# Reordering vector work and two state reads in a fused mLSTM and GELU kernel

## Chip, cores and metric

One Trainium2 chip, one core. The metric is the device time of one execution in microseconds (us); the median of 3 runs of the kernel before is 484.98 us (482.9 to 485.1). Engines are named as in the profile: PE is TensorE's matrix multiply, PEld its weight load, DVE VectorE, ACT ScalarE, POOL GpSimd, SP SyncE, whose queue starts all the transfers here.

## What is computed

The reference runs an mLSTM cell over q, k, v of shape (4, 8, 768, 40) with three gates, and feeds its output to a two-layer block with an exact GELU. Everything is float32.

```python
for t in range(S):                       # S = 768
    m_new = maximum(f + m, i)            # f, i: gates at t
    C = exp(f + m - m_new) * C + exp(i - m_new) * outer(v_t, k_t)
    n = exp(f + m - m_new) * n + exp(i - m_new) * k_t
    y[:, :, t] = sigmoid(o_t) * (C @ q_t) / maximum(abs(n . q_t), 1)
x = y.transpose(0, 2, 1, 3).reshape(3072, 320)
h = x @ w_in                             # 320 -> 2048
out = (0.5 * h * (1 + erf(h / sqrt(2)))) @ w_out   # 2048 -> 320
```

## The kernel before

**Chunks and stages.** The 768 steps are cut into NCH = 6 chunks of 128 steps; one chunk holds 4 batches b = 0 to 3 of 8 heads. Within a chunk the cell is a small attention: scores k·q, multiplied by a decay mask W that ACT makes with an exponential, times v (`values`), plus the carried state read with q and scaled by gT (`far`), and at the end of the chunk an update of the state. The 512 rows of x of a chunk then go through the up product into the hidden g (2048 x 512) and through the down product into the output.

After a front part (`FRONT`, to about 129 us) the kernel runs five stages, c = 1 to 5. Stage c does `up` for chunk c and then plays the order string `DOWN`: the 14 pieces of the down product of chunk c, mixed with the cell of chunk c + 1. The last stage has down pieces alone. The order is written by hand: each word of `DOWN` is a letter and a batch, and emits its instructions on the engines at that place. Each engine runs its own instructions strictly in that order.

**Letters** of `DOWN` that matter here:

- `F`: the next of 14 down pieces, 8 matmuls each (L888). Two pieces share one right-hand side. The scheme needs fewer than 16 products because sums of blocks of g stand in for blocks of g. Pieces 3 and 4 use the sums s2, pieces 7 and 8 the sums s1.
- `S0`, `S2`: scores of batches 0, 1 and of batches 2, 3 (`scores_two`): 64 small matmuls (L523) and 8 DVE multiplies of the scores into W (L529).
- `K`, `Q`: DVE transposes of k and q (L455); after `Q` the next batch's k and q are fetched by 16 transfers (L157), and POOL weighs v (L494).
- `C0`, `C2`: `carry_two`: 64 matmuls that read the state with q (L578), 32 that make its update (L585), then DVE's scaling of what was read (L594), POOL's decay of the state (L598) and DVE's addition of the update (L599).
- `V`: values (L617) and DVE's addition of them to what was read (L625). `V` of a batch loads W as weights, even heads first, odd heads after.
- `Y`: the division of the output by its norm (L630 on POOL, L632 to L635 on DVE). `X`: transposes of the output into x (L652), which need a copy of its last 64 columns, doubled (`y_rest`, L641); the copy for the next batch is made by DVE once `X` of this batch has read the present one. `R`: DVE splits x into two parts (L670, L671).
- `N`: `sum_late`, two DVE subtractions of 128x1024 that turn a block of g into a block difference (L918). It may run only after pieces 5 and 6 have read the block, and pieces 11 and 12 need it.
- `Z`: one step of the last weight sum T4, two DVE subtractions of 128x160 (L726); there are four, in stage 1 alone. Pieces 13 and 14 use T4.
- `M`, `W`, `G`, `L`, `D`, `B`, `j`: masks on POOL, exponentials and sigmoids on ACT, loads.

**up.** Four `pair` calls, 0 to 3, make the hidden pieces from x in three weight parts: w_hi, w_lo and their sum w_mid, which DVE joins anew in each stage (`join_weight`, L716). Each pair multiplies with w_hi, w_lo and w_mid in that order (L812); `rest` adds the last 64 rows of x (L823). ACT applies the GELU (L827). `hidden_sums(g, f0, f1)` is three DVE operations of 128x512 (L744 to L746) that form s1, s2 and a difference. After the GELUs of pairs 0 and 1 it is called for 0 to 2 and for 2 to 4; pair 3 then joins weights 8 and 9, and, in its `ahead` step, weight 7, which `rest(1, ...)` needs. One kind of joined weight (`w_in_mid`) has its own small buffers, so that the join for pair 3 may have to wait for an earlier pair's matmuls.

Of the kernel before, what the change touches and what calls it, by code (L numbers as in the profile page):

```python
# [9 lines left out]
F32 = mybir.dt.float32  # L10
# [6 lines left out]
P = 128  # L17
# [14 lines left out]
    Y1 T3 J J U U S3 V2 K K J G3 J Y2 C3 X0 K V3 J K F J F K K B8 F J K F F J K F F F R0 X1 J J K F J F K X2 F J K F  # L32
    J Y3 K F R1 J F Z B9 B10 F X3 R2 Z R3 F p"""
DOWN = """
    M0 Z M1 W0 F L3 F B3 W1 Z Z S0 F K2 C0 M2 G0 G1 G2 G3 V0 V1 W2 F Q2 K3 Q3 Y0 M3 D3 F F W3 F S2 F C2 V2 V3 j Z N F Y1
    X0 R0 Y2 F F X1 Y3 R1 F X2 R2 F X3 R3 F"""


@with_exitstack
def kernel(  # L40
# [18 lines left out]
    B, H, S, D = q.shape  # L59
    L = P  # L60
    NCH = S // L
    NP = H // 2
    D1 = D + 1
# [22 lines left out]
    ps_h = ctx.enter_context(tc.tile_pool(name="ps_h", bufs=2, space=bass.MemoryType.PSUM))  # L86
# [75 lines left out]
    def turn_of(n):  # L162

        return n % NLD if n < 2 * B else (n - 2 * B) % NQ
# [224 lines left out]
    def per_head(t, c, b):  # L389
        return t[:, c, b * H:(b + 1) * H].unsqueeze(2)  # L390

    class Cell:
# [173 lines left out]

            self.read(b)

        def carry_two(self, b0):

            c, two_b = self.c, (b0, b0 + 1)
            banks = [ps_h.tile([P, H + NP, D1], F32, name="pf", tag="h") for _ in range(2)]
            for i, b in enumerate(two_b):
                qT = self.qT.pop(b)
                for p in range(NP):
                    for r in halves:
                        for hip in range(2):
                            nc.tensor.matmul(banks[hip][r, NP * i + p, :], qT[halves[hip], p, r],  # L578
                                             state[b][halves[hip], p, 0:D1], start=True, stop=True)
            if c + 1 < NCH:  # L580
                for i, b in enumerate(two_b):
                    vw = self.vw.pop(b)
                    for p in range(NP):
                        for hip in range(2):
                            nc.tensor.matmul(banks[i][halves[hip], H + p, :], kb[turn_of(c * B + b)][:, 2 * p + hip, :],  # L585
                                             vw[:, 2 * p + hip, :], start=True, stop=True)
            for i, b in enumerate(two_b):
                if b == B - 1:
                    self.far[b] = qb[2].rearrange("p h d -> p (h d)")[:, 0:H * D1].rearrange("p (h d) -> p h d", d=D1)
                else:  # L590
                    self.far[b] = fars[0].tile([P, H, D1], F32, name="far", tag="hs", bufs=2)
                by_hip = lambda t, hip: t.rearrange("p (m two) d -> p m two d", two=2)[:, :, hip, :]
                for hip in range(2):
                    nc.vector.tensor_tensor(out=by_hip(self.far[b], hip), in0=banks[hip][:, NP * i:NP * i + NP, :],  # L594
                                            in1=by_hip(per_head(gT, c - 1, b), hip).to_broadcast([P, NP, D1]), op=OP.mult)
                if c + 1 < NCH:
                    st, d = state[b][:, :, 0:D1], dec[:, c - 1, b * NP:(b + 1) * NP].unsqueeze(2).to_broadcast([P, NP, D1])
                    nc.gpsimd.tensor_tensor(out=st, in0=st, in1=d, op=OP.mult)  # L598
                    nc.vector.tensor_tensor(out=st, in0=st, in1=banks[i][:, H:H + NP, :], op=OP.add)  # L599
                self.read(b)  # L600
# [113 lines left out]
    def join_weight(i):  # L714
        w_mid[i] = raw.tile([P, 2, WP // 2], F32R, name="w_in_mid", tag="pow") if i % 5 in (1, 4) else w_f(F32R, "w_mid")
        nc.vector.tensor_tensor(out=w_mid[i], in0=w_hi[i], in1=w_lo[i], op=OP.add)  # L716
# [22 lines left out]
    def hidden_sums(g, f0, f1):  # L739

        (a11, a21), (_, a22) = [[g.t[:, HF * e + f0:HF * e + f1, HT * h:HT * (h + 1)] for h in range(2)]
                                for e in range(2)]
        s1, s2 = [t[f0 // (HF // 2)][:, f0 % (HF // 2):f0 % (HF // 2) + f1 - f0, :] for t in (g.s1, g.s2)]
        nc.vector.tensor_tensor(out=s1, in0=a21, in1=a22, op=OP.add)  # L744
        nc.vector.tensor_tensor(out=s2, in0=s1, in1=a11, op=OP.subtract)
        nc.vector.tensor_tensor(out=a21, in0=a11, in1=a21, op=OP.subtract)  # L746
# [44 lines left out]
    def up(g, sums_too, turns):  # L791

        def split_to(i):
            while len(w_lo) <= i:
                split_weight()

        def pair(f, ahead):

            at = [f // 2 * 5 + f % 2 * 3 + x for x in range(NX)]
            split_to(at[1])  # L800
            for i in at:
                if i not in w_mid:
                    join_weight(i)
            pus = [[pool.tile([P, TG], F32, name="pu", tag=tag) for e in range(2)]
                   for pool, tag in (((ps_h, "h"), (ps_mm, "a")), ((ps_tr, "tr"), (ps_mm, "b")))[f % 2]]
            ahead()
            mid = [w_mid.pop(i) for i in at]
            for n, (w, x) in enumerate((([w_hi[i] for i in at], parts["x"]), ([w_lo[i] for i in at], parts["x_lo"]), (mid, parts["x_all"]))):
                for i in range(2):
                    for e in range(2):  # L810
                        for k in range(NX):
                            nc.tensor.matmul(pus[i][e], w[k][:, e, i * P:(i + 1) * P], x[:, k, :],  # L812
                                             start=(n == 0 and k == 0), stop=False, skip_group_check=True)
            return pus

        def rest(u, banks, order):
            mid = w_mid.pop(5 * u + 2)
            for i in order:
                pu = banks[i]
                for n, (w, x) in enumerate(((w_hi[5 * u + 2], parts["x"]), (w_lo[5 * u + 2], parts["x_lo"]), (mid, parts["x_all"]))):  # L820
                    for e in range(2):
                        r = halves[e]
                        nc.tensor.matmul(pu[e], w[r, i // 2, i % 2 * P:(i % 2 + 1) * P], x[r, NX, :], start=False,  # L823
                                         stop=(n == 2), skip_group_check=True)

        def out(i, e, pu):
            nc.scalar.activation(out=g.t[:, HF * e + i, :], in_=pu[e], func=AF.Gelu, scale=4097.0)  # L827

        b0 = pair(0, lambda: split_to(4))
        b1 = pair(1, lambda: join_weight(2))  # L830
        for step in turns[:1]:
            step()
        rest(0, b0 + b1, (0, 1, 2, 3))
        split_to(6)
        join_weight(5)
        join_weight(6)
        for i, pu in enumerate(b0 + b1):
            for e in range(2):
                out(i, e, pu)
        for step in sums_too[:5]:  # L840
            step()
        b2 = pair(2, lambda: split_to(9))
        hidden_sums(g, 0, 2)
        hidden_sums(g, 2, 4)
        b3 = pair(3, lambda: join_weight(7))
        for step in turns[1:] + sums_too[5:]:
            step()
        rest(1, b2 + b3, (2, 3, 0, 1))
        for i, e in ((2, 0), (2, 1), (3, 0), (0, 0), (1, 0), (3, 1), (0, 1), (1, 1)):
            out(4 + i, e, (b2 + b3)[i])  # L850
        hidden_sums(g, HF - 2, HF)
        hidden_sums(g, HF - 4, HF - 2)
# [100 lines left out]
    def cell_steps(c, letters, before=None):  # L953
        cell = Cell(c)
        cell.before = before
        return dict(zip(letters, (cell.mask, cell.weights, cell.gate, cell.turn, cell.scores, cell.carry, cell.values,
                                  cell.finish, cell.turn_y, cell.split_x, cell.load_last, cell.turn_k,
                                  cell.turn_q, cell.weigh_last, cell.carry_two,
                                  cell.last_M, cell.scores_two, cell.load_next)))

    first_g = Hidden(False)
    n_pieces = range(len(pieces))
# [8 lines left out]
    for c in range(1, NCH):  # L971
        g, later, steps = Hidden(True), [], {}
        if c + 1 < NCH:
            steps = cell_steps(c + 1, "MWGTscVYXRLKQDCBSj", g)
        up(g, weight_sum(1) + weight_sum(2) + weight_sum(3) if c == 1 else [], [lambda b=b: (steps["K"](b), steps["Q"](b)) for b in range(2)] if steps else [])
        if c == 1:
            later = weight_sum(4)
        products, late = down_steps(c, g)
        steps |= dict(F=in_turn(products), Z=in_turn(later), N=late)
        play("F " * 14 if c + 1 == NCH else DOWN, steps)  # L980
# [30 lines left out]
```

## Time and profile before

| | |
|---|---|
| median of 3 runs | 484.98 us (482.9 to 485.1) |
| profiled execution, own time | 483.16 us |
| its span, first to last instruction | 481.2 us |
| PE matmul / weight load busy | 473.1 us / 410.8 us |
| DVE / ACT / POOL busy | 351.5 / 222.2 / 73.7 us |
| granted TensorE clock | 1.000 |

Stages of the profiled execution, from the chain of waits (start of the up product, start of the first down piece, end), in us from the span's start:

| stage c | up starts | down starts | down ends | up | down |
|---|---|---|---|---|---|
| 1 | 129.33 | 158.27 | 203.07 | 28.94 | 44.80 |
| 2 | 203.07 | 231.65 | 275.89 | 28.58 | 44.24 |
| 3 | 275.89 | 304.48 | 348.39 | 28.59 | 43.91 |
| 4 | 348.39 | 376.99 | 418.85 | 28.60 | 41.86 |
| 5 | 418.85 | 447.43 | 478.07 | 28.58 | 30.64 |

Stages 1 to 3 hold the same number of matmuls; stage 4 lacks the 64 of the state update. An idle time in the profile is put down to the instruction that ended it ("PEld px L652 <- DVE y_rest L641" is PE's weight load waiting for a DVE copy). Ends of matmuls are modelled, so starts of weight loads are the better clock for PE.

### The profile page before, as it was taken

Reading aid. Unit: us, or ns where it says so; the run is one execution under the profiler, and the core shown is the slowest. Engines: PE = TensorE matmul, PEld = TensorE weight load, DVE = VectorE, ACT = ScalarE, POOL = GpSimd, SP = SyncE. Lnnn points to the kernel's source line nnn. Section 1 sums busy time; section 2 is a strip of 40 time slices with the busy share of each in tenths; the row PEclk is TensorE's granted clock in tenths of the full one; section 3 lists DMA queues with packets and bytes.
Section 4 is the critical chain, followed back from the end, with each engine's and each line's share of the span. In section 5 each row is a group of like instructions: output and inputs, shape, how many; then the busy total and the mean of one; then the engine's idle time right before and its main releaser. Section 6 shows DMA issues by size and latency. Waiting matters only on the chain.

```text
span 481.2 us, 11954 instructions
## 1 busy us (share of the span) xinstructions
PE 473.1 (98%) x4740; PEld 410.8 (85%) x4740; DVE 351.5 (73%) x762; ACT 222.2 (46%) x477; POOL 73.7 (15%) x104
## 2 busy tenths in 40 slices
PE   8899999999999999999999999999999999999997
PEld 7787888877777999877899977899977899977997
DVE  7899689797879988857488857488857488724321
ACT  6977999944532942113952103852104862112300
POOL 3001210000030234200136300135200213000000
PEclk9999999999999999999999999999999999999999
DMA  9998975289420368532257651257651250100001
GB/s 175 192 214 189 188 175 150 77 199 189 133 30 4 40 121 175 92 70 23 31 92 169 86 108 23 29 89 167 99 108 20 34 90 4 51 6 0 1 1 54
DMA packets 170423, 44.49 MB, mean 92 GB/s; under 512 B 156448, under 2 KB 163904, under 8 KB 170368
## 3 DMA queue, kind: packets, MB, share of 16 engines
q1 hardware_dynamic: 170368, 43.73, 46.4%
q8 instruction: 37, 0.61, 0.5%
q14 instruction: 18, 0.15, 0.1%
HBM read 39.58 MB, written 4.13 MB: 91 GB/s over the span
## 4 chain that ended last, share of the span: by engine, by line
PE 87%; DVE 7%; ACT 1%; SPq 1%; DMA 1%; issue 1%; DVEq 0%
PE po L888 30%; PE pu L812 22%; PE po L865 7%; PE pu L757 6%; PE pu L823 6%; PE ph L617 5%; PE ps L523 2%; PE pf L578 2%; PE pu L763 2%; PE px L652 2%; PE pf L585 1%; DVE g L918 1%; PE ps L507 1%; SPq L147 1%; PE pt L481 1%; ACT g L827 1%
## 5 line engine op out<-in xcount | busy, mean ns | idle before, releaser
L888 PE MATMUL po<-w_out,g 128*128 128x160 f32 x640 | 91.6, 301 | 0.0
L888 PEld LDWEIGHTS po<-w_out,g 128*128 128x128 f32 x640 | 87.9, 190 | 2.0 <-ACT g L827 1.8
L827 ACT ACTIVATE g<-pu 128x512 f32<-128x512 f32 x80 | 40.8, 614 | 53.4 <-PE pu L823 53.2
L888 PE MATMUL po<-w_sums,sums 128*128 128x160 f32 x320 | 47.7, 303 | 0.0
L888 PEld LDWEIGHTS po<-w_sums,sums 128*128 128x128 f32 x320 | 44.1, 190 | 0.7
L744 DVE TENSOR_TENSOR sums<-g 128x512 f32<-128x512 f32 x20 | 13.8, 690 | 38.5 <-ACT g L827 38.5
L812 PE MATMUL pu<-x_hi,w_in_hi 128*128 128x512 f32 x160 | 41.7, 403 | 0.0
L662 ACT ACTIVATE x_hi<-px 128x384 fp32r<-128x384 f32 x20 | 9.8, 489 | 67.8 <-PE px L652 67.8
L812 PE MATMUL pu<-x_lo,w_in_lo 128*128 128x512 f32 x160 | 40.6, 395 | 0.0
L432 ACT ACTIVATE W<-W,aT 128x128 f32<-128x128 f32 x128 | 39.2, 389 | 0.1
L812 PEld LDWEIGHTS pu<-x_hi,w_in_hi 128*128 128x128 f32 x160 | 28.5, 188 | 9.4 <-ACT g L827 4.1
L812 PEld LDWEIGHTS pu<-x_lo,w_in_lo 128*128 128x128 f32 x160 | 30.1, 188 | 7.2
L865 PE MATMUL po<-w_out,g 128*128 128x320 f32 x128 | 35.2, 433 | 0.0
L865 PEld LDWEIGHTS po<-w_out,g 128*128 128x128 f32 x128 | 24.0, 190 | 9.5
L827 ACT ACT_TABLE_LOAD x5 | 6.4, 1283 | 55.1 <-PE pu L823 41.3
L812 PE MATMUL pu<-x_all,w_in_mid 128*128 128x512 f32 x80 | 31.7, 396 | 0.1
L812 PE MATMUL pu<-x_all,w_mid 128*128 128x512 f32 x80 | 31.7, 396 | 0.0
L444 POOL MEMSET g<- 32x1024 f32 x8 | 7.6, 944 | 150.0 <-ACT W L432 149.8
L406 POOL TENSOR_SCALAR_AFFINE_SELECT W<-W 128x1024 f32<-128x1024 f32 (+2 forms) x20 | 21.8, 1100 | 55.4 <-DMA W<-M_d 55.1
L901 DVE TENSOR_TENSOR o_sb<-po,o_sb 128x320 f32<-128x320 f32 (+1 forms) x27 | 12.5, 465 | 23.9 <-PE po L888 19.9
L757 PE MATMUL pu<-first_x,w_in 128*128 128x256 f32 x128 | 29.1, 382 | 0.0
L757 PEld LDWEIGHTS pu<-first_x,w_in 128*128 128x128 f32 x128 | 23.8, 190 | 3.5 <-DVE w_in L374 0.4
(183 smaller groups left out, 910.0 us busy)
## 6 DMA issues: line engine op xcount, KB each, us to landing
W<-M_d SPq DMA_DIRECT2D x16, 512.0 KB, 5.7
bits<-in_moe_w_in_dram SPq DMA_DIRECT2D x20, 256.0 KB, 4.3
bits<-in_moe_w_out_dram SPq DMA_DIRECT2D x16, 320.0 KB, 3.2
ob<-in_o_gate_dram SPq DMA_DIRECT2D x24, 160.0 KB, 3.5
out_dram<-o_sb SPq DMA_DIRECT2D x24, 160.0 KB, 2.1
vb<-in_v_dram SPq DMA_DIRECT2D x14, 160.0 KB, 5.0
kb<-in_k_dram SPq DMA_DIRECT2D x14, 160.0 KB, 5.0
g<-M_d SPq DMA_DIRECT2D x4, 512.0 KB, 4.4
```

The source lines that it names most:

```text
L406: nc.gpsimd.affine_select(out=x, in_=x, compare_op=OP.is_ge, fill=1.0e30, base=base, pattern=[[0, H], [1, x.shape[2]]], channel_multiplier=-1)
L432: nc.scalar.activation(out=W[n][:, h, :], in_=src, func=AF.Exp, scale=-1.0, bias=aT[:, self.c, r:r + 1])
L617: nc.tensor.matmul(ph[r, h, :], Pm[:, h, r], vb[turn_of(n)][:, h, :], start=True, stop=True)
L662: nc.scalar.activation(out=parts["x"][:, :, t], in_=px, func=AF.Copy, scale=PART)
L744: nc.vector.tensor_tensor(out=s1, in0=a21, in1=a22, op=OP.add)
L757: nc.tensor.matmul(banks[-1][e][:, i - i0, :], in_tile(i, x)[:, e, i % 2 * P:(i % 2 + 1) * P], first_x[:, x, t0:t1], start=(x == 0 and i = ...
L812: nc.tensor.matmul(pus[i][e], w[k][:, e, i * P:(i + 1) * P], x[:, k, :], start=(n == 0 and k == 0), stop=False, skip_group_check=True)
L823: nc.tensor.matmul(pu[e], w[r, i // 2, i % 2 * P:(i % 2 + 1) * P], x[r, NX, :], start=False, stop=(n == 2), skip_group_check=True)
L827: nc.scalar.activation(out=g.t[:, HF * e + i, :], in_=pu[e], func=AF.Gelu, scale=4097.0)
L865: nc.tensor.matmul(po[b], g.t[:, f, b * L:(b + 1) * L], w_out[:, f, :], start=(f == 0), stop=(f == NF - 1))
L888: nc.tensor.matmul(bank[at][:, i, :], lhs(j, t), rhs(j), start=(first and i == 0 and j == 0), stop=(i == n - 1 and j == HF - 1), skip_grou ...
L901: nc.vector.tensor_tensor(out=to, in0=pb, in1=x, op=OP.add)
```

## The change

Three parts. In `DOWN` the late sums `N` go from behind `j` to ahead of `W3` and `S2`, and the last `Z` goes from ahead of `N` to behind `X1`. `carry_two` is cut into a reading half (`C`) and an updating half (new letter `h`); for batches 0 and 1 the third down piece `F`, which stood between `S0` and `C0`, now stands between `C0` and `h0`; for batches 2 and 3 `h2` follows `C2` directly. In `up` the second `hidden_sums` goes into pair 3's `ahead` step, so that the joins of weights 8 and 9 come ahead of it and the join of weight 7 still behind it.

```diff
 DOWN = """
-    M0 Z M1 W0 F L3 F B3 W1 Z Z S0 F K2 C0 M2 G0 G1 G2 G3 V0 V1 W2 F Q2 K3 Q3 Y0 M3 D3 F F W3 F S2 F C2 V2 V3 j Z N F Y1
-    X0 R0 Y2 F F X1 Y3 R1 F X2 R2 F X3 R3 F"""
+    M0 Z M1 W0 F L3 F B3 W1 Z Z S0 K2 C0 F h0 M2 G0 G1 G2 G3 V0 V1 W2 F Q2 K3 Q3 Y0 M3 D3 F F N W3 F S2 F C2 h2 V2 V3 j F Y1
+    X0 R0 Y2 F F X1 Z Y3 R1 F X2 R2 F X3 R3 F"""
...
-        def carry_two(self, b0):
+        def read_two(self, b0):
...
-            banks = [ps_h.tile([P, H + NP, D1], F32, name="pf", tag="h") for _ in range(2)]
+            banks = self.banks = [ps_h.tile([P, H + NP, D1], F32, name="pf", tag="h") for _ in range(2)]
...
                             nc.tensor.matmul(banks[hip][r, NP * i + p, :], qT[halves[hip], p, r],
                                              state[b][halves[hip], p, 0:D1], start=True, stop=True)
+
+        def update_two(self, b0):
+
+            c, two_b, banks = self.c, (b0, b0 + 1), self.banks
             if c + 1 < NCH:
...
         hidden_sums(g, 0, 2)
-        hidden_sums(g, 2, 4)
-        b3 = pair(3, lambda: join_weight(7))
+        b3 = pair(3, lambda: (hidden_sums(g, 2, 4), join_weight(7)))
```

No instruction is added or removed on any engine. On PE only the eight matmuls of piece 3 change place, on DVE the joins, `N` and one `Z`; the orders on ACT, POOL and SP are the same.

More of the change, by code (lines that the diff above doesn't have):

```diff
@@ L957, in cell_steps @@
                                   cell.finish, cell.turn_y, cell.split_x, cell.load_last, cell.turn_k,
-                                  cell.turn_q, cell.weigh_last, cell.carry_two,
-                                  cell.last_M, cell.scores_two, cell.load_next)))
+                                  cell.turn_q, cell.weigh_last, cell.read_two,
+                                  cell.last_M, cell.scores_two, cell.load_next, cell.update_two)))
     first_g = Hidden(False)
@@ L973 @@
         if c + 1 < NCH:
-            steps = cell_steps(c + 1, "MWGTscVYXRLKQDCBSj", g)
+            steps = cell_steps(c + 1, "MWGTscVYXRLKQDCBSjh", g)
         up(g, weight_sum(1) + weight_sum(2) + weight_sum(3) if c == 1 else [], [lambda b=b: (steps["K"](b), steps["Q"](b)) for b in range(2)] if steps else [])
```

## The prediction

> **What bounds the kernel now.** The page first: PE is busy for nearly the whole span, and the chain that ended last is mostly PE.
>
> ```profile
> PE 473.1 (98%) x4740; PEld 410.8 (85%) x4740; DVE 351.5 (73%) x762; ACT 222.2 (46%) x477; POOL 73.7 (15%) x104
> ...
> PE 87%; DVE 7%; ACT 1%; SPq 1%; DMA 1%; issue 1%; DVEq 0%
> ```
>
> As no matmul is removed, the change can only take out places where PE waits. The waits of the weight loads, with total, count and longest in us, bound that from above:
>
> ```profile
> PEld pu L812 <- ACT g L827: 4.1, 17, 0.4
> PEld pu L823 <- issue: 3.7, 10, 0.4
> ...
> PEld pf L578 <- issue: 1.4, 8, 0.2
> PEld px L652 <- DVE y_rest L641: 1.3, 3, 0.8
> ```
>
> The first two are GELU outputs and a change of shape that the change leaves alone. The last two it touches. A third is only in the answer for the joining line L716, as who waited for it:
>
> ```profile
> PEld pu L812: 0.7, 2
> ```
>
> Where do these lie? The stage table says that stage 1 is longer than stage 3 by 28.94 - 28.59 = 0.35 us in the up part and 44.80 - 43.91 = 0.89 us in the down part, stage 2 by 0.33 us in the down part. So 1.57 us is what bringing stages 1 and 2 to stage 3 is worth. The timeline of DVE and of the weight loads shows the down part's cause, in stages 1 and 2:
>
> ```profile
> 187.50 0.50 DVE L625 TENSOR_TENSOR qb<-ph,qb 128x328 f32<-128x328 f32 x1 [0.19 <-PE ph L617]
> 187.91 1.37 DVE L726 TENSOR_TENSOR t<-w_out,w_sums 128x160 f32<-128x160 f32 x2
> 189.21 2.89 DVE L918 TENSOR_TENSOR g<-g,sums 128x1024 f32<-128x1024 f32 x2
> ...
> 194.43 0.93 DVE L641 COPY y_rest<-ob 128x128 f32<-128x128 f32 x1
> ...
> 195.41 0.14 PEld L652 LDWEIGHTS px<-ident,y_rest 128*128 128x128 f32 x1 [0.76 <-DVE y_rest L641]
> ...
> 268.23 0.14 PEld L652 LDWEIGHTS px<-ident,y_rest 128*128 128x128 f32 x1 [0.37 <-DVE y_rest L641]
> ```
>
> From V3's end DVE runs Z, N and Y1 without rest, and X1 waits for the copy behind them: 0.76 and 0.37 us. In stages 3 and 4 the copy is just in time and nothing waits.
>
> [...] N takes 2.89 us in stage 1 and 3.17 us in stage 2, where POOL's multiplies lie beside it and last up to 1.79 us instead of 0.81. [...] the shortest L918 is 1212. The next operation starts 0.08 us before one's end, so an undisturbed pair costs DVE 2.27 us. [...] The trace shows 0.17 to 0.18 us of idle before a 64*64 group that follows a 128*128 one:
>
> ```profile
> 240.00 1.02 PEld L578 LDWEIGHTS pf<-state,qT 64*64 64x64 f32 x64 [0.17 <-issue]
> 241.07 1.01 PEld L585 LDWEIGHTS pf<-vw,kb 128*64 128x64 f32 x32
> ```
>
> **Part 1, N and Z out of the tail.** After V3 they take 1.30 + 2.81 = 4.1 us of DVE in stage 1 and 3.1 us in stages 2 to 4. Both waits of X1 are shorter than that, so both go: 0.76 + 0.37 = 1.13 us, of which about 0.1 is ordinary spacing (stage 3 has 0.26 us from the first load of X1 to the copy's load, stages 1 and 2 have 0.97 and 0.65): -1.0 us, between -0.9 and -1.1. Z now sits between X1 and X2 of stage 1: two operations of 0.24 us apart, before the copy for X3, which has some 1.5 us to spare once the tail has drained. Zero; were that wrong, X3 would wait 0.5 us at most.
>
> What N now delays is S2's eight multiplies L529, and through them V2 and V3. Stage 4 is the tightest:
>
> ```profile
> 397.51 0.57 DVE L641 COPY y_rest<-ob 128x128 f32<-128x128 f32 x1
> 398.96 1.41 DVE L529 TENSOR_TENSOR W<-ps,W 128x256 f32<-128x256 f32 x4 [0.88 <-PE ps L523]
> 400.29 1.76 DVE L529 TENSOR_TENSOR g<-ps,g 128x256 f32<-128x256 f32 x4
> ...
> 403.16 1.02 PEld L617 LDWEIGHTS ph<-vb,g 128*64 128x64 f32 x32
> ```
>
> DVE is free at 398.0 (end of the copy less 0.08) and stood idle until 398.96. N from 398.0 ends its hold at 400.27, so L529 starts 1.31 us late. V3's odd heads are loaded at 403.62 and need the last L529, which ended at 402.05: slack 1.57. The same reading gives:
>
> | stage | DVE free | L529 began | delay by N alone | slack of V3 |
> |---|---|---|---|---|
> | 1 | 180.42 | 181.18 | 1.51 | 2.50 |
> | 2 | 253.70 | 254.56 | 1.41 | 2.41 |
> | 3 | 326.79 | 327.38 | 1.68 | 2.50 |
> | 4 | 398.00 | 398.96 | 1.31 | 1.57 |
>
> One POOL operation of 0.74 to 0.81 us (L494, in stage 4 L630) falls beside N in each stage; [...] half of it is my value. Then stages 1 to 3 still fit (1.8 to 2.1 against 2.4 to 2.5) and stage 4 is short by 0.1 to 0.2: +0.15 us, between 0 and +0.7. V2 has over 2.3 us everywhere. N itself does not wait: piece 6 ended at about 250.7 in stage 2, 3 us before DVE is free. Behind L529, DVE's L901, L594 and L625 come up to 2 us later, but without N behind them Y1 still starts earlier: in stage 2 near 262.3 instead of 264.4. POOL's L630 of Y2 waits for L625 and its next products move about 1.4 us; X2 needs them 6 us later. The banks that the late operations free are next wanted by the next up.
>
> **Part 2, piece 3 behind the reads.** PE has the same matmuls between S0 and V0, so V0 comes no later. The modes go 64*64, 64*64, 128*128, 128*64 instead of 64*64, 128*128, 64*64, 128*64: one change fewer. Half of L578's waits go, 0.17 us in each of four stages = 0.7; the load behind piece 3 would pay about 0.17 where L585 had 0.05, 0.1 x 4 back. I take -0.4 us, between 0 and -0.75. The reads' inputs are there: they are those of S0, and the banks were freed at 233.8, before 237.6. POOL's L598 may start 2.4 us earlier and then its mask; its weighing of v still waits for L585. DVE reaches L594 at the same time as before, behind L529 and K2.
>
> **Part 3, joins between the sums.** In stage 1 the joins start at 152.05, behind six operations of the sums; pair 3 wants them at 152.6 and waits 0.20 and 0.37 us (spacing of the loads above normal). Three of the six, 1.9 us, go behind them: -0.57 us, between -0.35 (the table's excess) and -0.6. Join 7 ends as before, at 153.9, and is wanted near 155.0. In stages 2 to 4 pair 3 does not wait, and there DVE now does: in stage 2 the join of weight 9 must wait for PE until 223.09, so the second sums slip from 220.5 to 223.7, join 7 from 223.7 to 225.6 (wanted at 228.9) and the transposes K1, Q1 by 1.9 us. Their 16 transfers L157 then leave SP from 227.7 to 235.5 instead of from 225.8 to 233.6; SP's next work starts at 236.9, and the last landing moves from 236.3 to about 238.2, wanted at 241.8. Zero; a transfer that slips more would show as S2 late, whose k and q are ready 1.3 to 1.5 us ahead.
>
> **Sum.** -1.0 + 0.15 - 0.4 - 0.57 = -1.8 us. On the profiled execution: 483.16 to 481.3, with the span from 481.2 to 479.4. The median shown is 484.98, 1.8 us above the profiled execution, as the runs lie in 482.9 to 485.1; the same saving gives 483.2 us.
>
> **The rivals.**
>
> *All small terms go well.* With -1.1, 0, -0.75 and -0.6 the saving is 2.45 us, 482.5 us; a DVE tail without N might also mend spacing that I could not see, 0.5 us more: 482.0. For it: PE has no other wait there. Against it: stage 3 shows what an undisturbed stage costs.
>
> *The waits move, not vanish.* Stage 1's saved 0.57 us is lost to the next GELU wait (L812 on L827 has 4.1 us in all) and the mode change costs the same in its new place; with 0.7 us of V3 waits only 0.3 us is left, 484.7 us. For it: DVE in stage 1 works through to 165.4 on weight sums with no rest.
>
> *N makes V3 the bound.* If N in its new place is stretched more than beside POOL today, the slack of all four stages is gone. The savings of 1.95 us are used up when N takes about 3.5 us instead of 2.27 to 2.7: the delays are then 2.5 to 2.9 and the waits 0.24 + 0.23 + 0.41 + 0.97 = 1.9. At 4.2 us they are 4.6 us, and the time is 484.98 + 2.6 = 487.6 us. Against it: the longest N in the trace is 3.25 us, with three POOL operations beside it, and here there is one.
>
> **How the numbers follow.** A measurement of this kernel can tell about 0.5%, or 2.4 us, from no change. The main case, 483.2 us (482.6 to 484.2), has 0.6; all going well 0.17; waits moved 0.12; V3 as the bound 0.11. Runs of one kernel differ by up to 2 us, so the main case ends beyond 0.5% at times: faster 0.3, same 0.58, slower 0.12. The range 481.4 to 485.3 takes in the first three cases and leaves out the slow one and the edges.
>
> **What would show it.** Right: no weight load of L652 waits for L641 in stages 1 and 2; no wait for L716; the down part of stages 1 and 2 at 43.8 us like stage 3; L578 without idle in its first place; L918 starting near 180.4, 253.7, 326.8 and 398.0 and lasting 2.3 to 3.0 us. Wrong: loads of L617 for V3 that wait for L529 beyond stage 4, S2 late behind its transposes, or a new wait for L827.

## The result, and the profile after

| kernel | median us | runs |
|---|---|---|
| before | 483.5 (482.4 to 487.3) | 22 |
| after | 481.28 (480.2 to 485.9) | 22 |

The ratio is 0.9952, with a 95% interval of 0.9935 to 0.9970: the change saves 2.2 to 2.3 us, 0.48%. The interval excludes a change of zero. With 22 runs the kernel before stands at 483.5, not at the 484.98 of its first three. An execution with a mean granted clock of 0.996 or less typically took over 1 us longer (of the 47 runs of before made beside e1 below, the 12 such took 484.2 us or more and the other 35 at most 483.9), and their share goes from none of e10's six runs to four of e4's six, so that medians of few runs are rough. The span goes from 481.2 to 479.0 us, 2.2 less, at a granted clock of 1.000 in both.

The page of after, in the lines that answer to those shown of before:

```profile
span 479.0 us, 11954 instructions
...
PE 470.5 (98%) x4740; PEld 410.1 (86%) x4740; DVE 351.5 (73%) x762; ACT 222.2 (46%) x477; POOL 70.4 (15%) x104
...
PE 78%; issue 10%; DVE 7%; SPq 2%; DMA 1%; ACT 1%; POOL 0%; DVEq 0%; POOLq 0%
```

The counts are the same and PE is as full as it was. The chain (the work that ended last, followed back) looks different, 78% of PE where it had 87%, but the 9 points are now called "issue", time for which the profile names no wait: together they are 88%, as before. Such a shift between names is not a change of the bound.

The waits of the weight loads in after (total, count, longest, in us; before's L812, L823, L652 and L641 are L816, L827, L656 and L645 here, L888 and L918 are L891 and L921):

```profile
PEld pu L816 <- ACT g L831: 4.1, 17, 0.4
PEld pu L827 <- issue: 3.6, 10, 0.4
...
PEld pf L578 <- issue: 0.7, 4, 0.2
```

The first two are untouched. L578 is down from eight waits to four. The wait of L652 for the copy, 1.3 us before, is no longer among the large ones; the profile has one load left that waited for the copy, line L645, and that lies ahead of the stages:

```profile
  PEld px L656: 0.2, 1
```

**By stage.** Starts of weight loads cut each stage into stretches. The table gives the stretches that moved, before, and after minus before, in us; "values" is from V2's first load to the piece behind V3. The other stretches agree within 0.02.

| stretch | stage 1 | stage 2 | stage 3 | stage 4 |
|---|---|---|---|---|
| second half of up | 14.80, -0.44 | 14.43, 0 | 14.43, 0 | 14.43, 0 |
| S0 to V0 | 5.87, -0.16 | 5.87, -0.16 | 5.87, -0.16 | 4.94, -0.16 |
| values of 2 and 3 | 2.00, 0 | 2.00, 0 | 2.00, 0 | 2.00, +0.56 |
| piece behind V3 to X1 | 7.06, -0.24 | 6.82, 0 | 6.88, -0.06 | 6.82, 0 |
| X1 to X2 | 3.18, -0.67 | 2.85, -0.35 | 2.48, +0.03 | 2.50, 0 |
| X2 to X3 | 2.58, -0.07 | 2.58, -0.07 | 2.58, -0.08 | 2.50, 0 |
| X3 to the next up | 2.58, -0.08 | 2.58, -0.08 | 2.58, -0.07 | 2.50, 0 |
| sum of the differences | -1.68 | -0.65 | -0.34 | +0.40 |

In all -2.27: joins -0.44, change of modes -0.63, the tail (the four rows that name an X) -1.75, V3 of stage 4 +0.56; each number is rounded by itself. A mode here is the shape that the profile gives behind the operands of each weight load: 128*128, 64*64 or 128*64 in the lines below.

The weight loads of the tail of stage 1 in after (start, duration, both in us):

```profile
193.60 0.28 PEld L656 LDWEIGHTS px<-ident,ob 128*128 128x128 f32 x2
193.85 0.14 PEld L656 LDWEIGHTS px<-ident,y_rest 128*128 128x128 f32 x1
193.96 2.20 PEld L891 LDWEIGHTS po<-w_out,g 128*128 128x128 f32 x16
196.11 0.28 PEld L656 LDWEIGHTS px<-ident,ob 128*128 128x128 f32 x2
196.35 0.14 PEld L656 LDWEIGHTS px<-ident,y_rest 128*128 128x128 f32 x1
```

From an X's first load to the load of its copy it is 0.25 us, where X1 had 0.97 before. The same view at the first group of stage 1:

```profile
162.31 1.43 PEld L523 LDWEIGHTS ps<-qT,kT 64*64 64x64 f32 x64 [0.17 <-issue]
163.64 1.03 PEld L578 LDWEIGHTS pf<-state,qT 64*64 64x64 f32 x64
164.72 2.20 PEld L891 LDWEIGHTS po<-w_sums,sums 128*128 128x128 f32 x16
167.09 1.01 PEld L589 LDWEIGHTS pf<-vw,kb 128*64 128x64 f32 x32 [0.17 <-POOL state L602]
```

The reads follow the scores without idle, and the idle of 0.17 us that L578 had behind the piece is now L589's. At pair 3 of stage 1:

```profile
152.59 0.19 PEld L816 LDWEIGHTS pu<-x_all,w_mid 128*128 128x128 f32 x1
152.82 0.19 PEld L816 LDWEIGHTS pu<-x_all,w_in_mid 128*128 128x128 f32 x1
```

The two waits for joined weights are gone. What the change costs stands in stage 4; here is DVE ahead of V3:

```profile
393.00 0.17 DVE L636 TENSOR_SCALAR den<-far 128x8 f32<-128x8 f32 x1
393.21 1.06 DVE L637 SCALAR_TENSOR_TENSOR den<-far,den 128x8 f32<-128x8 f32 x1
...
395.33 0.72 DVE L645 COPY y_rest<-ob 128x128 f32<-128x128 f32 x1
395.98 2.35 DVE L921 TENSOR_TENSOR g<-g,sums 128x1024 f32<-128x1024 f32 x2
398.25 1.40 DVE L529 TENSOR_TENSOR W<-ps,W 128x256 f32<-128x256 f32 x4
399.58 1.76 DVE L529 TENSOR_TENSOR g<-ps,g 128x256 f32<-128x256 f32 x4
```

and PE, whose V3 waits for the last of these multiplies. The profile marks 0.18 us at its even heads and 0.20 at its odd ones; against the starts of before it is about 0.26 and 0.31, the 0.56 of the table:

```profile
400.61 0.58 PEld L621 LDWEIGHTS ph<-vb,g 128*64 128x64 f32 x16 [0.18 <-issue]
401.39 0.55 PEld L621 LDWEIGHTS ph<-vb,g 128*64 128x64 f32 x16 [0.20 <-DVE g L529]
```

N takes 2.35 us, two operations of 1.21 us each, and before's shortest L918 is 1212 ns. It starts late: the small L637 of Y0 took 1.06 us, six times the 0.17 that it took in before, and the copy L645 took 0.72, where the median of its 24 is 0.23. In before the same small operation started 0.02 us ahead of POOL's first mask of `W3` and took 0.17 us:

```profile
396.01 0.17 DVE L633 SCALAR_TENSOR_TENSOR den<-far,den 128x8 f32<-128x8 f32 x1
```

```profile
396.03 1.97 POOL L406 TENSOR_SCALAR_AFFINE_SELECT g<-g 64x1024 f32<-64x1024 f32 x2 [5.09 <-DMA g<-M_d]
```

### The profile page after: what moved, and what is told of

It is laid out like the page before. It is cut to its first block, busy times and chain, and to the rows that moved or that the text cites. A ratio compares the mean times of both kernels' runs of the same rounds, so it can differ in the third digit from the quotient of the medians.

```text
span 479.0 us, 11954 instructions
## 1 busy us (share of the span) xinstructions
PE 470.5 (98%) x4740; PEld 410.1 (86%) x4740; DVE 351.5 (73%) x762; ACT 222.2 (46%) x477; POOL 70.4 (15%) x104
## 4 chain that ended last, share of the span: by engine, by line
PE 78%; issue 10%; DVE 7%; SPq 2%; DMA 1%; ACT 1%; POOL 0%; DVEq 0%; POOLq 0%
PE po L891 27%; PE pu L816 19%; PE po L868 7%; PE pu L761 5%; PE pu L827 5%; PE ph L621 4%; PE ps L523 2%; PE pu L767 1%; PE pf L589 1%; SPq L147 1%; PE px L656 1%; PE pf L578 1%; PE ps L507 1%; SPq L157 1%; PE pt L481 1%
## 5 line engine op out<-in xcount | busy, mean ns | idle before, releaser
L891 PE MATMUL po<-w_out,g 128*128 128x160 f32 x640 | 91.6, 301 | 0.0
L891 PEld LDWEIGHTS po<-w_out,g 128*128 128x128 f32 x640 | 87.7, 190 | 2.0 <-ACT g L831 1.8
L891 PE MATMUL po<-w_sums,sums 128*128 128x160 f32 x320 | 47.7, 303 | 0.0
L891 PEld LDWEIGHTS po<-w_sums,sums 128*128 128x128 f32 x320 | 44.1, 190 | 0.7
L816 PE MATMUL pu<-x_hi,w_in_hi 128*128 128x512 f32 x160 | 41.7, 402 | 0.0
L816 PE MATMUL pu<-x_lo,w_in_lo 128*128 128x512 f32 x160 | 40.6, 395 | 0.0
L816 PEld LDWEIGHTS pu<-x_hi,w_in_hi 128*128 128x128 f32 x160 | 28.5, 188 | 9.3 <-ACT g L831 4.1
L816 PEld LDWEIGHTS pu<-x_lo,w_in_lo 128*128 128x128 f32 x160 | 30.1, 188 | 7.2
L720 DVE TENSOR_TENSOR w_in_mid<-w_in_hi,w_in_lo 128x512 fp32r<-128x512 f32 x20 | 13.8, 688 | 24.4 <-PE pu L816 24.4
L816 PE MATMUL pu<-x_all,w_mid 128*128 128x512 f32 x80 | 31.6, 395 | 0.0
L816 PE MATMUL pu<-x_all,w_in_mid 128*128 128x512 f32 x80 | 31.6, 395 | 0.0
```

What stands on the lines that cost most here:

```text
L891: nc.tensor.matmul(bank[at][:, i, :], lhs(j, t), rhs(j), start=(first and i == 0 and j == 0), stop=(i == n - 1 and j == HF - 1), skip_grou ...
```

## The experiments

| kernel | median us (runs) | before beside it (runs) | ratio, 95% interval |
|---|---|---|---|
| e1, joins alone | 482.63 (14) | 483.41 (47) | 0.9990, 0.9976 to 1.0004 |
| e2, reads alone | 482.86 (22) | 483.41 (47) | 0.9989, 0.9973 to 1.0005 |
| e3, sums alone | 481.75 (18) | 483.41 (47) | 0.9969, 0.9953 to 0.9984 |
| e4, reads ahead in both groups | 481.18 (6) | 483.41 (47) | 0.9947, 0.9930 to 0.9964 |
| e5, Y0 behind S2 | 481.35 (8) | 483.30 (27) | 0.9952, 0.9934 to 0.9970 |
| e6, e4 and e5 | 480.32 (5) | 483.30 (27) | 0.9928, 0.9905 to 0.9952 |
| e7, N back | 481.82 (17) | 483.30 (27) | 0.9974, 0.9962 to 0.9986 |
| e8, Z back | 481.04 (8) | 483.30 (27) | 0.9961, 0.9936 to 0.9986 |
| e9, N back in stage 4 | 480.54 (17) | 483.47 (22) | 0.9941, 0.9924 to 0.9958 |
| e10, e4 and e9 | 479.62 (6) | 483.47 (22) | 0.9913, 0.9882 to 0.9944 |

The profiled executions of e1, e2, e3, e4 and e9 reach stage 1 by 1.0 to 3.8 us later than that of before, so the kernels are compared below by the stretches of stages 1 to 4 and not by their spans. Differences are against before unless after is named.

**e1: the joins alone.** Before, with one edit:

```diff
-        hidden_sums(g, 2, 4)
-        b3 = pair(3, lambda: join_weight(7))
+        b3 = pair(3, lambda: (hidden_sums(g, 2, 4), join_weight(7)))
```

> Only part 3: in up, the second hidden sums go behind the joins of weights 8 and 9; order string and carry_two as before. Theory (parts add, each worth what PE's loads show): in stage 1 the last rows of x (L823) start 0.44 us earlier than before, and all of PE behind them is 0.44 us earlier to the end; stages 2 to 5 gain nothing; -0.44 us, 483.1 us against 483.5. Rival (the wait moves): PE meets another wait behind it, the down part of stage 1 or the next GELU wait grows, and less than 0.15 us is left at the end.

The second half of up in stage 1 is 0.44 us shorter, to the hundredth what after shows; S0 to V3 are unchanged everywhere. The time alone, whose interval takes in 1, doesn't settle it. One thing was not expected: in this execution X1 of stage 1 came 1.36 us later behind the piece, and 0.70 of that came back ahead of X2. DVE there:

```profile
190.19 3.43 DVE L917 TENSOR_TENSOR g<-g,sums 128x1024 f32<-128x1024 f32 x2
193.54 1.05 DVE L632 TENSOR_SCALAR den<-far 128x8 f32<-128x8 f32 x1
194.62 1.00 DVE L633 SCALAR_TENSOR_TENSOR den<-far,den 128x8 f32<-128x8 f32 x1
```

and POOL, whose masks lie beside it:

```profile
191.35 1.18 POOL L494 TENSOR_TENSOR vw<-vb,ewT 128x328 f32<-128x328 f32 x1 [0.49 <-DMA vb<-in_v_dram]
192.49 3.83 POOL L406 TENSOR_SCALAR_AFFINE_SELECT W<-W 128x1024 f32<-128x1024 f32 x3
```

N, L917 in this kernel, is 3.43 us long, where it took 2.89 in before, and two operations of 0.16 and 0.17 us grow to 1.05 and 1.00. Beside these two run POOL's masks, three in 3.83 us; before's trace has a single one of this size, at 241.69 us, with 1.09. So an operation of 128x8 took nearly as long here as a mask. That the masks are the cause is read from the times; why they would be is not shown. POOL's start hangs on the landing of a transfer (v here: POOL stood 0.49 us before L494, and 2.32 in before's stage 1), so before's X1 wait of 0.76 us is one value among several: here it was near 1.5. In the old order a little time won in up can be lost again in the tail, and in this execution all of it was: stages 1 to 4 together are 0.23 us longer than before's.

**e2: the reads alone.** Before, with `carry_two` split as in the change and the order

```diff
-    ... S0 F K2 C0 ... S2 F C2 V2 V3 ...
+    ... S0 K2 C0 F h0 ... S2 F C2 h2 V2 V3 ...
```

> Only part 2: piece 3 between the reads and the update of the first group; N, Z and up as before. Theory (one change of tiling mode fewer): [...] 0.16 us is gained between S0 and V0 in each of stages 1 to 4, -0.63 us in all, 482.9 us. Rival (the gain comes from POOL and DVE being let go earlier): S0 to V0 is as long as before, and the 0.16 us does not show in this kernel or shows in other places.

S0 to V0 is 0.16 us shorter in each of the four stages, and nothing else moves but X1 of stage 1 (+0.80, then -0.43), the same wait as in e1. So with N and Z in the old order the tail of stage 1 took 15.4 us in before's trace, 15.8 in e2's and 16.1 in e1's; with N moved it is 14.3 in after, e3, e4, e8, e9 and e10. The waits of L578 halve and three of 0.17 us appear at L589, a fourth at the values of stage 4, which has no update: the marked idle only changes its owner. The gain is in the spacing of the starts, which carries no mark. From S0's first load to the next group it was 1.50 us with the piece behind it and is 1.33 with the reads (162.31 to 163.64 above); the piece costs 2.37 to the next group in either place.

**e3: the sums alone.** N and Z at their new places, the rest as before (`carry_two` is split in the code, but `C0 h0` and `C2 h2` stand side by side):

```diff
-    ... D3 F F W3 F S2 F C2 V2 V3 j Z N F Y1
-    X0 R0 Y2 F F X1 Y3 ...
+    ... D3 F F N W3 F S2 F C2 h2 V2 V3 j F Y1
+    X0 R0 Y2 F F X1 Z Y3 ...
```

> Only part 1: N ahead of S2, last Z behind X1; first group and up as before. Theory (all three copies for X1, X2, X3 were late before, X2 and X3 by 0.06 us or so each, and in stage 4 V3 waits now): the tail from X1 to the end of the down part gains about 1.0 us in stage 1, 0.5 in stage 2, 0.2 in stage 3, nothing in stage 4, and V3 of stage 4 loses 0.2 to 0.6: -1.1 to -1.5 us, 482.2 us. Rival (only X1 waited, as I predicted; the small gains belong to the other parts): 1.0 us in stages 1 and 2 together and none in stage 3: with V3's wait -0.4 to -0.8 us.

The tail is shorter by 1.06, 0.49 and 0.18 us in stages 1 to 3, the numbers of after, and S0 to V0 and up are unchanged. By the ratios the three parts alone add up to 0.52%, and the whole is 0.48%. V3 of stage 4 waits 0.20 us, where after has 0.56. Its DVE (N is L922 here) and its POOL:

```profile
398.07 0.17 DVE L637 SCALAR_TENSOR_TENSOR den<-far,den 128x8 f32<-128x8 f32 x1
...
400.01 2.80 DVE L922 TENSOR_TENSOR g<-g,sums 128x1024 f32<-128x1024 f32 x2
```

```profile
398.88 2.86 POOL L406 TENSOR_SCALAR_AFFINE_SELECT g<-g 64x1024 f32<-64x1024 f32 x2 [5.88 <-DMA g<-M_d]
```

and in after, POOL:

```profile
393.16 1.81 POOL L406 TENSOR_SCALAR_AFFINE_SELECT g<-g 64x1024 f32<-64x1024 f32 x2 [4.87 <-DMA g<-M_d]
```

In after the mask starts 0.05 us ahead of L637, which then takes 1.06 us; in e3 it starts 0.8 us behind it, and L637 takes 0.17. Counted from S2's first load:

| | first mask starts | N starts | V3 waits in all |
|---|---|---|---|
| after | -1.32 | 1.50 | 0.56 |
| e4 | -1.50 | 1.37 | 0.60 |
| e3 | -0.46 | 0.67 | 0.20 |
| e8 | -0.57 | 0.68 | 0.21 |

The mask waits for a transfer (`g<-M_d`; POOL stands 4.87 us before it in after, 5.88 in e3). Where it lands early, Y0's chain on DVE is stretched, N starts 0.7 to 0.8 us later, and V3 pays 0.4. This is a pattern of four executions; the transfer's landing was not moved by itself, so the cause is argued from the times and not shown.

**e4: the second group in the same order.** After, with

```diff
-    ... S2 F C2 h2 V2 V3 ...
+    ... S2 C2 F h2 V2 V3 ...
```

> The changed kernel, and piece 8 also between the reads and the update of the second group (S2 C2 F h2). Theory (mode changes cost 0.16 us each): another 0.16 us in each of stages 1 to 4 between S2 and V2, -0.63 us against the changed kernel: 480.65 us, -2.85 against the kernel before. Rival (the first group's gain came from POOL's earlier release, which the second group does not lack): no difference from the changed kernel, 481.3 us.

S2 to V2 is 0.16 us shorter in each stage, in addition to S0 to V0. PE in stage 4, where S2's reads follow its scores by 1.33 us:

```profile
394.90 1.43 PEld L523 LDWEIGHTS ps<-qT,kT 64*64 64x64 f32 x64 [0.17 <-DVE den L637]
396.23 1.03 PEld L578 LDWEIGHTS pf<-state,qT 64*64 64x64 f32 x64
397.31 2.20 PEld L891 LDWEIGHTS po<-w_sums,sums 128*128 128x128 f32 x16
```

So the 0.16 us goes with the order of modes and not with a batch or with POOL's earlier release: the second group has it too, and stage 4, with no update of the state, has it in both. In these traces two groups of 64*64 side by side save 0.16 to 0.17 us against a 128*128 piece between them; what PE does in that time is not shown. The median, 0.1 us under after's, can't show a gain of 0.6: the six runs lie between 480.1 and 481.9.

**e5: Y0 behind S2,** so that N needn't wait for it. After, with

```diff
-    ... Q3 Y0 M3 D3 F F N W3 F S2 F C2 h2 ...
+    ... Q3 M3 D3 F F N W3 F S2 Y0 F C2 h2 ...
```

> The changed kernel with Y0 (division of batch 0's output, on DVE and POOL) moved from ahead of N to behind the products of S2. Theory (V3 of stage 4 waits because [...] N starts late; N itself is not stretched): N starts as soon as the transposes end, about 1.5 us ahead of S2, the products of S2 start where they did in the kernel before (1.67 us after S2's first load), V2 and V3 take 2.00 us again instead of 2.56, and X0 to X3 keep their 2.50 us: -0.55 us against the changed kernel, 480.75 us. Rival (the two late sums are themselves too long for the place): the sums meet the masks instead, end 2.5 us after S2's first load or later, and V3 still waits.

The gain did not come: V3 still waits 0.61 us and the time is that of after. N did start early, 1.2 us ahead of S2's first load, but then:

```profile
393.61 2.36 DVE L921 TENSOR_TENSOR g<-g,sums 128x1024 f32<-128x1024 f32 x2
...
399.91 1.78 DVE L529 TENSOR_TENSOR g<-ps,g 128x256 f32<-128x256 f32 x4 [2.01 <-POOL ob L634]
```

```profile
394.97 2.67 POOL L406 TENSOR_SCALAR_AFFINE_SELECT g<-g 64x1024 f32<-64x1024 f32 x2 [11.82 <-DMA g<-M_d]
```

```profile
397.67 2.44 ACT L432 ACTIVATE g<-g,aT 128x128 f32<-128x128 f32 x8 [4.51 <-POOL g L406]
```

Now N is first: POOL's two masks of W3 start under N's second operation and take 2.67 us instead of the 1.81 of after, ACT's exponentials start late behind the masks, and the multiplies of batch 3 stand until 399.91 for their W. (The profile names L634, but that had ended at 399.30; the seventh of the eight exponentials ended at 399.83.) Here it is POOL's work that grows beside DVE's, by 0.86 us, where in after and e1 it was DVE's beside POOL's. That is only part of it: the mask's transfer also came late, so that the mask starts 0.18 us behind S2's first load where after has it 1.32 ahead. The move has a price of its own besides: Y0's work on DVE now lies ahead of the tail, and in stage 1 X3's load of the copy waits 0.27 us.

**e6: e4 and e5 together.** After, with

```diff
-    ... Q3 Y0 M3 D3 F F N W3 F S2 F C2 h2 ...
+    ... Q3 M3 D3 F F N W3 F S2 Y0 C2 F h2 ...
```

> The changed kernel with both: Y0 behind S2's products, and piece 8 between the reads and the update of the second group. Theory (the terms add): -0.55 and -0.63 us against the changed kernel, 480.1 us, -3.4 us against the kernel before. Rival: Y0's operations now lie between S2's products and the values, the update of the state or V2's addition comes late, and PE waits for a bank or for W in V2 or in X0: no better than the kernel with both groups alone.

V3 of stage 4 waits 0.22 us and the mode changes give 0.16 in all eight places, but V3 of stage 2 waits 0.14, and from X2 to the next up 0.51 us more than in after go in stage 1 and 0.27 in stage 2. Stages 1 to 4 come to -2.30 us, where after has -2.27 and e4, the same kernel without Y0's move, -2.91. So in these traces the rival holds: e6 is no better than e4, and Y0's move is not the remedy. The medians lean the other way (480.32 against 481.18), but with five and six runs and intervals that overlap they don't settle it; e6's traced execution, 480.64, is the slowest of its five.

**e7: N back, Z still behind X1.** After, with

```diff
-    ... F F N W3 ... V3 j F Y1
+    ... F F W3 ... V3 j N F Y1
```

> The changed kernel with N back behind j (the last Z stays behind X1). Theory (N in the tail is what made X1 late; Z only added in stage 1): V3 of stage 4 takes 2.00 us again; stage 2 has its wait of 0.35 us at X1 and the 0.07 to 0.08 us at X2, X3 back, stage 3 its 0.2 us; stage 1, with 1.3 us less of Z in the tail, waits 0 to 0.3 us at X1: 0.8 to 1.1 us of waits return and 0.56 go, +0.3 to +0.5 us against the changed kernel, 481.7 us. Rival (Z alone carries the gain of the tail): equal to the changed kernel in stage 1 and faster over all by 0.5 us.

V3 of stage 4 waits no more (+0.00), and the tails of stages 2 and 3 are those of before to 0.01 us: N made both the gain and the cost. In stage 1, where Z no longer precedes N, X1 keeps its gain, but X2 and X3 pay for the copies that come late behind N and Z:

```profile
196.54 0.14 PEld L656 LDWEIGHTS px<-ident,y_rest 128*128 128x128 f32 x1 [0.20 <-DVE y_rest L645]
...
199.12 0.20 PEld L656 LDWEIGHTS px<-ident,ob 128*128 128x128 f32 x2 [0.32 <-issue]
199.59 0.14 PEld L656 LDWEIGHTS px<-ident,y_rest 128*128 128x128 f32 x1 [0.27 <-DVE y_rest L645]
```

X2 to X3 grows by 0.48 us. The whole is 0.5 us over after by the medians and 0.9 by the stages (-1.38 against -2.27). Z behind X1 is free only if N has left the tail.

**e8: Z back, N moved.** After, with

```diff
-    ... V2 V3 j F Y1
-    X0 R0 Y2 F F X1 Z Y3 ...
+    ... V2 V3 j Z F Y1
+    X0 R0 Y2 F F X1 Y3 ...
```

> The changed kernel with the last Z back behind j (N stays ahead of S2). Theory: without N the tail of stage 1 has some 2 us to spare, Z's 0.5 to 1.4 us fit, and every stage is as in the changed kernel: 481.3 us, no difference. Rival (Z in the tail still makes X1 late in stage 1): X1 of stage 1 waits 0.3 us or more.

All stretches are those of after within 0.03 us but V3 of stage 4 (+0.21, told above). Z's move is worth nothing once N is gone.

**e9: N back in stage 4 alone,** where the tail has nothing to gain. After, with

```diff
-        play("F " * 14 if c + 1 == NCH else DOWN, steps)
+        order = DOWN.replace(" N W3", " W3").replace(" j F", " j N F") if c + 2 == NCH else DOWN
+        play("F " * 14 if c + 1 == NCH else order, steps)
```

> The changed kernel, but in stage 4 alone N stands in its old place behind j, as the tail of stage 4 had no late copy. Theory (V3 of stage 4 waits only because of N ahead of S2's products, and the tail of that stage has room for N): V2 and V3 of stage 4 take 2.00 us instead of 2.56, X0 to X3 keep 6.82 and 2.50 us, stages 1 to 3 are as in the changed kernel: -0.55 us against it, 480.75 us. Rival (the wait comes from where POOL's masks fall, whatever N does): V3 of stage 4 waits 0.2 us or more again.

V3 of stage 4 is at 2.00 us and the tail there at 6.82, 2.50, 2.50, 2.50: both at their least. DVE shows the multiplies waiting for PE again, and N behind V3:

```profile
397.62 1.41 DVE L529 TENSOR_TENSOR W<-ps,W 128x256 f32<-128x256 f32 x4 [0.91 <-PE ps L523]
...
403.60 3.44 DVE L921 TENSOR_TENSOR g<-g,sums 128x1024 f32<-128x1024 f32 x2
```

480.54 us against 481.28 of after, by the ratios 0.11%; the intervals overlap. That the gain is the 0.56 us of V3 is shown by the trace alone.

**e10: e4 and e9 together.** The code of e9, and in `DOWN`

```diff
-    ... S2 F C2 h2 V2 V3 ...
+    ... S2 C2 F h2 V2 V3 ...
```

> The same, and piece 8 between the reads and the update of the second group as well. Theory (the terms add): 0.16 us less from S2 to V2 in each of stages 1 to 4 besides, -1.2 us against the changed kernel, 480.1 us, -3.4 us (0.7%) against the kernel before. Rival: with the updates of the second group later, V2 or the next stage finds a bank or W late, and no more than 0.3 us of the 0.63 is left.

479.62 us, 0.87% under before, and the interval of 0.9882 to 0.9944 lies all but wholly below that of after: the best version. The stages give -1.81, -0.83, -0.51 and -0.34, in all -3.5 us, and the span is 477.7. The waits of the weight loads name the reads L578 no more; what is left of the modes is behind the pieces:

```profile
PEld pf L589 <- issue: 0.7, 4, 0.2
```

The medians put e10 1.66 us under after, the stages 1.2. The interval covers both, and the trace shows no source for the rest.

## Why the prediction was right or wrong

It forecast 483.2 us with no measurable change as likeliest; it is 481.28, 1.9 us lower and under the range's 481.4. The signs held, and the mechanisms in the main. Two steps failed, and their errors add up: the base was 1.5 us too high, and the sum came out 0.4 to 0.5 us too small, above all in the term for the tail.

**The base.** The larger of the two is "the same saving gives 483.2 us": the saving was subtracted from the median of three, 484.98, though the profiled execution beside it read 483.16. Before's median over 22 runs is 483.5, and 483.5 - 1.8 = 481.7, which is inside the range; the forecast for the profiled execution itself, span 479.4, was 0.4 us off the 479.0 that came. Of the 22 runs 15 lie under 484 us and 7 at 484.5 or more; two of the first three were among the 7, so their median was a high one. The profiled execution lay with the 15, and I set it aside.

**Part 1, the tail: -1.75, not -1.0.** That N's 2.4 us and more in the tail made X1 wait, and that both waits go, is right (e3; in e7 the wait of stage 2 is back with N). The mis-sized term is "of which about 0.1 is ordinary spacing" together with the yardstick, "stage 3 shows what an undisturbed stage costs". Stage 3 was disturbed itself: before's stage 4 had 2.50 us from X to X where stage 3 had 2.58, in the trace on which the prediction rests. DVE and PE of before at X3 of stage 3 show why:

```profile
345.62 0.22 DVE L641 COPY y_rest<-ob 128x128 f32<-128x128 f32 x1
```

```profile
345.52 0.28 PEld L652 LDWEIGHTS px<-ident,ob 128*128 128x128 f32 x2
345.88 0.14 PEld L652 LDWEIGHTS px<-ident,y_rest 128*128 128x128 f32 x1
```

The copy ends at 345.84 and its load goes at 345.88, 0.36 us after X3's first instead of 0.25: a wait of 0.1 us that the profile doesn't mark. So where the prediction reads "the copy is just in time and nothing waits", there was a wait. In after the copy of that X3 ends at 341.40, 1.5 us ahead. Against stage 4's stretches the prediction would have had 1.08 + 0.51 + 0.20 = 1.8 us. The move of Z cost nothing, as said, and won nothing once N was gone (e8). That the gain of stage 1 came out at 1.06 us is in part chance: against the tails of e1 and e2 the same tail of after would be 1.7 and 1.4 us shorter.

**N ahead of S2: +0.56 in stage 4, not +0.15.** That stages 1 to 3 have the slack and stage 4 is the one to fall short held to the stage; V2 never waits. The slack was read rightly too: L529 began 2.10 us later than before, counted from S2's first load (3.77 us behind it instead of 1.67), 0.53 over the slack of 1.57, and V3 waits 0.56. What was wrong is the delay. One POOL operation, "half of it is my value", was an estimate of what N itself would lose. N lost nothing, with 2.35 us for the pair (1.21 each); the stretched operations are those of Y0 and the copy ahead of it, which the table of "DVE free" took as fixed. From S2's first load, N was to start at about 0.7 and started at 1.50. The result lies within the term's bound of +0.7, so the size was rightly left open and its value chosen too low. In e3 and e8 N does start at 0.67 and 0.68, and V3 waits 0.20, where my +0.15 is nearly right. The rival "N makes V3 the bound" needs about 3.5 us of N: behind Y0 and ahead of S2 it took 2.92 at most (e4, stage 3). It took over 3.5 us only in e6, 3.73 in stage 3, where it starts 1.5 us ahead of S2 and V3 does not wait.

**Part 2: -0.63, not -0.4.** One change of mode fewer is right, and its price is 0.16 us in each of four stages. The sum got there by the wrong terms: it took L578's marked waits as the gain and gave 0.1 back at the update. The marked idle is given back in full (0.17 at L589 for 0.17 at L578); the gain lies in the start of the group behind the scores, 1.33 us instead of 1.50, which no mark shows. e4 repeats it in the other group.

**Part 3: -0.44, not -0.57.** Both waits for L716 are gone and nothing waits in stages 2 to 4, as said. The row of marked waits, 0.20 + 0.37, was 0.13 us more than what came back, as PE had made that much up by itself: in before the load behind the second wait follows it by 0.11 us, where 0.23 is usual. The other bound, the table's excess of stage 1 over stage 3 of 0.35, was 0.09 too small. Second halves of up now measure 14.36 in stage 1 and 14.43 in the others.

**Steps put at nothing** that did cost nothing: the 16 transfers that leave SP later, POOL's shifted work, DVE's work behind L529. S2 to V2 is 5.87 us in stages 1 to 3, as before. Y1 in stage 2 was to start 2.1 us earlier; it starts at 260.61 instead of 264.39, of which 1.84 is PE's own lead by then, so 1.9.

**The rivals.** "All small terms go well", 482.0 to 482.5, had the saving nearly right at its lower end (2.45 us against 2.2 to 2.3), and one of its reasons is what came: the tail without N mended spacing that had not been seen. Its time missed by the same base. "The waits move" is true of V3 in stage 4 alone.

## What to carry to other kernels

Where stages repeat, compare like stretches across all of them, take the shortest with the same work as the yardstick, and read an excess of under 0.1 us between starts as a wait until the producer's end is shown to lie well ahead; marks of idle time tell who waited, and not what a reorder is worth. Move vector work off the path only in stages where it is on the path: in the last cell stage the old place was free, and keeping it there won back what the new place cost. Before a saving is subtracted from a median of a few runs, compare it with the profiled execution's own time; where the two differ by as much as the saving, the base is not known yet.

## What the runs showed of the hardware

- A DVE operation of 128x8 that takes 0.16 or 0.17 us took 1.06 us (L637 in after) and 1.05 and 1.00 us (e1) beside POOL masks of 1.1 us or so, and two POOL masks that take 1.81 us in after took 2.67 in e5, where they started under a DVE operation of 1.2 us. The loss was 0.83 to 0.89 us each time: five times its own length for a small operation, about half of theirs for the two masks.
- Two neighbouring groups of 64*64 matmuls save 0.16 to 0.17 us against a 128*128 group between them, in eight places of e4 alike. From 64*64 to 128*64 the next load starts 0.05 to 0.06 us behind the last one's end, in before and after, and the profile marks no wait.
- POOL's first mask of `W3` starts with the landing of a transfer, and POOL stood 4.87 us for it in after and 5.88 in e3. Against PE's own progress that start lay between 1.50 us ahead of S2 and 0.46 ahead in four kernels (after, e3, e4 and e8), and where it was early the DVE chain ran 0.7 to 0.8 us later. A wait of 0.2 or of 0.6 us in one profiled execution may be this alone; no run moved the landing by itself.
